# Sliding-block attention mixed with a Fourier layer: the value sums of four key blocks in one visit to the small array tiles

## The chip, the cores and the metric

The kernel runs on one core of a Trainium2 chip. The metric is the device time of one execution in microseconds. A core has a matrix engine (PE, with its weight loads listed as PEld), VectorE (DVE), ScalarE (ACT), GpSimd (POOL) and a queue (SP) that here issues all transfers. The array of PE can work as one tile of 128 by 128 or as small tiles, for instance four of 128 rows by 32 columns that run side by side. PSUM is the small memory into which PE writes.

## What is computed

There are two branches over the same 2048 rows of 512 numbers, mixed by a gate for each row. Branch A is a Fourier layer written as matrix products; branch B is attention with 32 heads of 16 numbers, in which a query sees the 256 keys up to itself.

```
a = x @ hid_re.T;  b = x @ hid_im.T
A = seq_re @ a - seq_im @ b                       # 2048 x 2048 matrices
q, k, v = split(x @ wqkv)                         # 32 heads of 16
scores = q @ k.T * 16**-0.5, kept where 0 <= i - j < 256
B = concat(softmax(scores) @ v) @ wo
g = sigmoid(sum(x * gate_w))
out = g * A + (1 - g) * B
```

## The kernel before

All data is float32. The dense products are made exact enough by splitting each operand into a high and a low part and adding three products (`TERMS`, line 212), each a matmul of 128 by 128 weights with 512 columns. They form one long stream of work (`dense`, line 479): projections of q and k (L238), of v (L260, tile dv), of a and b (L260, tile dab), then the sums over the sequence (`c_chunk`, L442, tile dc). The stream is a Python generator that gives out one matmul at a time.

Attention is cut into `NG` = 4 groups of 8 heads and `NB` = 32 blocks of 64 rows, so 128 blocks in all. A block's heads are handled in `NP` = 4 pairs, two heads at once by a block-diagonal "pad" of 128 columns. Attention has three passes:

- The score pass, `s_pair(n, p)` (line 309): for query block n and pair p a matmul of 128 by up to 320 (L319); DVE adds the mask and takes the extreme of each row (L321); ACT takes the exponential and sums it (L324). Only the row's extreme `nm` and sum `l` are kept; the exponentials in tile `sm` are thrown away. `sm` has three buffers.
- The transposed pass, `t_pair(k, p)` (line 377): for key block k and pair p a matmul (L384) of the same kind with the extreme already subtracted, since it stands in extra rows 96 to 99 of `ring[0]`; ACT takes the exponential into tile `pt` (L385), and POOL clears the two corners outside the band (L390, L394). `pt` holds the four pairs of one key block, and has three buffers.
- The value sums, `pv(n)` (line 397): for key block n and each of the four pairs a matmul with 32 weight columns (L411) into 32 partitions of a PSUM tile `o`. The four run on four small tiles of the array. Where the 320 queries of a block cross a border of 512, the block takes two rounds of four. In the trace each of these float32 matmuls stands twice. After the last key block of a 512 the result is multiplied by the reciprocal sum (`rl`, L421) and stored.

The weights of the value sums come from tile `vpad`, where v of four blocks (a group of four) lies spread out with zeros between: `v_load` fetches it into `vr` by two transfers of 64 KB, `v_spread` spreads it on POOL (L374, two copies). `vpad` has two buffers, `vr` two.

The pads are made by `make_pad` (line 293) from the ring of q or k: two DVE operations for a score pad, one DVE (L304) and one ACT operation (L302) for a transposed pad. There are `NPAD` = 3 buffers of each kind.

Every eighth block `m_rows` and `l_rows` turn the extremes and sums of eight blocks into rows, by a matmul with the identity each (L331, L343, 32 columns, small tiles too), DVE copies (L334, L335, L345) and transfers through memory. The extremes go to rows 96 to 99 of `ring[0]`, where the transposed pass reads them later.

The main loop (lines 645 to 681) runs over n. In iteration n it makes the scores of block n and the transposed pass of block k = n - `LAG` with `LAG` = 18, one pair of each for p = 0 to 3, and calls `fill(n)` twice for each p, which takes 1.5 to 1.8 matmuls of the dense stream. In every odd n, at p = 2, it calls `pv` for blocks k - 2 and k - 1: that is one visit to the small tiles, for two key blocks. `m_rows` and `l_rows` follow at n % 8 == 1, in the same place. After the loop the rest of the dense stream runs, with the last product by wo (L604).

The order of PE's instructions is the order of these calls, written out by hand (`manual_schedule`, line 639). On DVE, ACT, POOL and SP a planner sets the order: it may move an instruction up as soon as its inputs and its buffer are free by its own reckoning, except where `behind(...)` holds it after an earlier one. Each engine then works strictly in its order. The tiles `s` and `t` in PSUM share four buffers (`ps_a`), the dense results have two (`ps_d`), `o` has two (`ps_o`). The pool `ev` has five buffers for tiles of 128 by 512, used for results on the way to or from memory.

Of the kernel before, what the change touches and what calls it, by code (L numbers as in the profile page):

```python
# [7 lines left out]
F32 = mybir.dt.float32  # L8
# [6 lines left out]
P = 128  # L15
# [3 lines left out]
NG = 4  # L19
NP = 4  # L20
BQ = 64
NB = S // BQ
WIN = 320
BIG = 1e30
SCALE = 0.25
LAG = 18
# [5 lines left out]
def fnet_window_mix(ctx: ExitStack, tc: tile.TileContext, xT, x, wqk, wv, wr, wi, cr, ci, wo, gw, out):  # L32
    nc = tc.nc

    const = ctx.enter_context(tc.tile_pool(name="const", bufs=1))
    big = ctx.enter_context(tc.tile_pool(name="big", bufs=16))
    st = ctx.enter_context(tc.tile_pool(name="st", bufs=3))
    ev = ctx.enter_context(tc.tile_pool(name="ev", bufs=5))
    at = ctx.enter_context(tc.tile_pool(name="at", bufs=2))
# [14 lines left out]
    def ld(dst, src):  # L54
        return nc.sync.dma_start(dst, src)
# [4 lines left out]
    def f(ap):  # L60
        return ap.bitcast(F32)
# [4 lines left out]
    def mark(e, ins):  # L66
        last[e] = ins.ins

    @contextmanager
    def behind(*engines):  # L70
        with ExitStack() as es:
            for e in engines:
                if e in last:
                    es.enter_context(tc.issue_after(last[e]))
            yield
# [46 lines left out]


    def pt_raw():
        return at.tile([P, NP, WIN], F32, name="pt", bufs=3).rearrange("p a b -> p (a b)")[:, :1024]

    with tc.manual_schedule(engines={mybir.EngineType.Activation, mybir.EngineType.DVE, mybir.EngineType.SP}):
        wraw, *xraw = [pt_raw() for _ in range(3)]
# [5 lines left out]
        for dk in range(DK):  # L134
            c = slice(dk * 256, dk * 256 + 256)
# [2 lines left out]
            nc.vector.tensor_sub(wq0[1][:, c], wraw[:, c], f(wq0[0][:, c]))  # L138


    NPAD = 3
    pads = [[const.tile([P, NP, P], F32R, name=f"pad{i}_{b}") for b in range(NPAD)] for i in range(2)]
    ring = [const.tile([P, NP, S], F32R, name=f"ring{i}") for i in range(2)]

# [15 lines left out]
    for t, edges in ((half, ((0, 16, 32, 48, 64, 80), (16, 32, 48, 64, 80, 96))), (mrow, ((96, 98), (98, 100)))):  # L160
        nc.gpsimd.memset(t, 0.0)
        for h in range(2):
            for i, e in enumerate(edges[h]):
                a = t[:, h:h + 1]
# [3 lines left out]
    def clear_rows(i, ss):  # L168
        nc.gpsimd.memset(f(ring[i][96:128, :, ss * 512:(ss + 1) * 512]), 0.0)
# [2 lines left out]
        nc.gpsimd.memset(f(t[96:128]), 0.0)  # L172
    clear_rows(1, 0)
    clear_rows(0, 0)
    vpad = [const.tile([P, 4, NP, 32], F32, name=f"vpad{b}") for b in range(2)]

    def clear_pads():
        for t in vpad:
            nc.gpsimd.memset(t, 0.0)
        for t in pads[1]:  # L180
            nc.gpsimd.memset(f(t[96:128]), 1.0)
            for h in range(2):
                a = t[96:128, :, 64 * h:64 * h + 64]
                nc.vector.tensor_scalar(a, f(a), mrow[96:128, h:h + 1], None, op0=OP.mult)
# [108 lines left out]
    def make_pad(i, n):  # L293
        if not 0 <= n < NG * NB:
            return
        t = pads[i][n % NPAD]
        b = n % NB
        with behind(*(("act", "dve") if n < NPAD else ())):
            for h in range(2):
# [9 lines left out]
    def s_pair(n, p):  # L309
        j = n % NB  # L310
        u, jj = divmod(n, 8)
        if jj == 0 and p == 0:
            ML[u] = [at.tile([P, NP * 8], F32, name="nm"), at.tile([P, NP * 8], F32, name="l")]
        nm, l = ML[u]
        k0 = max(0, (j - 4) * BQ)
        w = (j + 1) * BQ - k0
        c = slice(p * 8 + jj, p * 8 + jj + 1)
        ps = ps_a.tile([P, 512], F32, name="s", tag="st")
        nc.tensor.matmul(ps[:, :w], PAD[0, n][:, p], ring[1][:, p, k0:k0 + w], start=True, stop=True)  # L319
        sm = at.tile([P, WIN], F32, name="sm", bufs=3)  # L320
        mark("dve", nc.vector.tensor_tensor_reduce(out=sm[:, :w], in0=ps[:, :w], in1=mask[:, WIN - w:],  # L321
                                                   scale=1.0, scalar=3e38, op0=OP.add, op1=OP.min,
                                                   accum_out=nm[:, c]))
        mark("act", nc.scalar.activation(sm[:, :w], sm[:, :w], AF.Exp, bias=nm[:, c], scale=-1.0,  # L324
                                         accum_out=l[:, c]))
# [23 lines left out]
               lt[:, 64 * a:64 * a + 64])  # L349

    OT = {}
    V2 = {}
    PT = {}

    VR = {}

    def v_load(n):
        if n >= NG * NB:
            return
        g, kb = divmod(n, NB)  # L360
        raw = at.tile([P, 4, 64], F32, name="vr")
        for h in range(2):
            ld(raw[64 * h:64 * h + 64].rearrange("r (c j) x -> r c j x", j=2),
               v_scr[kb // 4][:, :, h, g, :].rearrange("c (j r) x -> r c j x", r=64))
        VR[n] = raw

    def v_spread(n):
        if n >= NG * NB:
            return
        raw = VR.pop(n)  # L370
        v2 = vpad[n // 4 % 2]
        for h in range(2):
            r = slice(64 * h, 64 * h + 64)
            nc.gpsimd.tensor_copy(v2[r, :, :, 16 * h:16 * h + 16], raw[r].rearrange("r j (p d) -> r j p d", d=16))  # L374
        V2[n // 4] = v2

    def t_pair(n, p):
        q0 = n % NB * BQ
        w = min(WIN, S - q0)
        if p == 0:  # L380
            PT[n] = at.tile([P, NP, WIN], F32, name="pt", bufs=3)
        pt = PT[n]
        ps = ps_a.tile([P, 512], F32, name="t", tag="st")
        nc.tensor.matmul(ps[:, :w], PAD[1, n][:, p], ring[0][:, p, q0:q0 + w], start=True, stop=True)  # L384
        nc.scalar.activation(pt[:, p, :w], ps[:, :w], AF.Exp, scale=-1.0)  # L385
        if p % 2:
            ph = slice(p - 1, p + 1)
            for h in (0, 64):
                a = pt[h:h + 64, ph, 0:64]
                nc.gpsimd.affine_select(a, a, pattern=[[0, 2], [1, 64]], compare_op=OP.is_ge, fill=0.0,  # L390
                                        base=0, channel_multiplier=-1)
                if w == WIN:
                    a = pt[h:h + 64, ph, 256:320]
                    nc.gpsimd.affine_select(a, a, pattern=[[0, 2], [-1, 64]], compare_op=OP.is_gt, fill=0.0,  # L394
                                            base=0, channel_multiplier=1)

    def pv(n):
        g, kb = divmod(n, NB)
        v2 = V2[n // 4][:, n % 4]
        pt = PT.pop(n)  # L400
        q0 = kb * BQ
        w = min(WIN, S - q0)
        q = q0
        while q < q0 + w:
            sb = q // 512
            e = min(q0 + w, (sb + 1) * 512)
            first = (g, sb) not in OT
            if first:
                OT[g, sb] = ps_o.tile([P, 512], F32, name="o")
            for p in range(NP):  # L410
                nc.tensor.matmul(OT[g, sb][32 * p:32 * p + 32, q - sb * 512:e - sb * 512], v2[:, p],  # L411
                                 pt[:, p, q - q0:e - q0], start=first, stop=kb == 8 * sb + 7,
                                 skip_group_check=True)
            q = e
        if kb % 8 == 7:
            sb = kb // 8
            ps = OT.pop((g, sb))
            rl = at.tile([P, 512], F32, name="rl", bufs=1)
            ls = l_scr[g * 4 + sb]
            ld(rl, bass.AP(tensor=ls.tensor, offset=ls.offset, ap=[[512, 2 * NP], [0, 16], [1, 512]]))  # L420
            nc.vector.tensor_mul(rl, ps, rl)  # L421
            ld(o_scr[sb][g], rl)
# [190 lines left out]
    def need(key):  # L613
        while key not in have:
            next(stream)
# [15 lines left out]
    def fill(n):  # L631
        nonlocal quota
        rate = FILL_FIRST if n < LAG else FILL_SEQ if "proj" in have else FILL_PROJ
        quota += rate / 2
        while quota >= 1:
            next(stream, None)
            quota -= 1

    ctx.enter_context(tc.manual_schedule(engines={mybir.EngineType.PE}))
    N = NG * NB  # L640
# [1 line left out]
    ring_ahead(0)  # L642
    need(("v", 5))

    for n in range(N + LAG + 2):
        if n in (1, 3, 5):
            for i in range(2):
                clear_rows(1 - i, (n + 1) // 2)
        if n == 7:
            clear_pads()  # L650
        k = n - LAG
        ring_ahead(n + 1)
        if -4 <= k < N - 4 and k % 4 == 0:
            for c in range(2):
                need(("v", (k + 4) % NB // 2 + c))
            with behind(*(("sp",) if k < 4 else ())):
                v_load(k + 4)
        if -4 <= k and k % 4 == 2:
            v_spread(k + 2)
        if n == 0:  # L660
            make_pad(0, 0)
        if k == 0:
            make_pad(1, 0)
        for p in range(NP):
            if n < N:
                s_pair(n, p)
            fill(n)
            if 0 <= k < N:
                t_pair(k, p)
            if p == 0:  # L670
                make_pad(0, n + 1)
                if k >= 0:
                    make_pad(1, k + 1)
            fill(n)
            if p == 2 and n % 2:
                for j in (k - 2, k - 1):
                    if 0 <= j < N:
                        pv(j)
                if n % 8 == 1 and 1 < n <= N + 1:
                    m_rows(n // 8 - 1)  # L680
                    l_rows(n // 8 - 1)
    attention_done()
# [46 lines left out]
```

## Time and profile before

| | us |
|---|---|
| median of 3 runs | 880.83 (879.98 to 882.15) |
| the profiled execution, its own time | 881.33 |
| its span | 879.5 |
| granted clock of PE, mean | 0.996 |
| ACT busy, 110 to 300 us (190 us) | 165.69 |
| ACT busy, 300 to 660 us (360 us) | 291.65 |
| ACT busy, 660 to 760 us (100 us) | 44.77 |

The profiled execution is 0.50 us above the median and 1.8 us longer than its span. The score pass ends at 669 us, the transposed pass at 752 us, and the value sums at 758 us; what follows is dense work alone. Engine rows give busy time in us, the share of the span, and the number of instructions; a group row gives line, engine, operation, tiles and shape, the count, and then busy us, mean ns of one, and the engine's idle time before them. A timeline row gives start, length, engine, line, operation, tiles and shape, and what the engine waited for, if it was idle. A matmul's length includes its way through the array, so that the next one starts before it ends: what a matmul costs PE is the distance from its start to the next start.

### The profile page before, as it was taken

The page shows a single profiled execution, that of the slowest core. Times are in us where ns is not written, and L with a number is a line of the kernel's source. Part 1 is how long each engine was busy: PE and PEld are TensorE (multiplying, and loading weights), DVE is VectorE, ACT ScalarE, POOL GpSimd, SP SyncE. Part 2 cuts the span into 40 slices and gives each one's busy share as a digit, 9 for nine tenths or more (in the row PEclk, how much of TensorE's full clock was granted, in tenths as well). Part 3 has the DMA queues.
Part 4 walks back from the last instruction along what each step waited for, and adds up shares of the span by engine and source line. Part 5 has one row for each costly group of instructions (what it writes and reads, how often), then busy time and mean ns, then how long its engine had stood idle before and what let it go on. Part 6 is the DMA issues. An engine that isn't in the chain of part 4 may idle for free.

```text
span 879.5 us, 17216 instructions
## 1 busy us (share of the span) xinstructions
PE 866.5 (99%) x5184; PEld 692.2 (79%) x5184; DVE 600.1 (68%) x1965; ACT 585.3 (67%) x1794; POOL 385.0 (44%) x1069
## 2 busy tenths in 40 slices
PE   7999899999999999999999999999999999999997
PEld 6888678777877878787778787877878777788885
DVE  4688788777887677777777777778776443454342
ACT  5488788889888887888878878888776444100010
POOL 9100165555544447564455566545656664000000
PEclk9999899999999999999999999999999999999999
DMA  7877668775766136543544353579643323455452
GB/s 265 261 228 214 198 205 272 233 237 174 221 207 210 45 99 200 147 138 120 175 131 140 127 148 115 143 230 348 211 143 126 130 92 126 137 174 156 149 159 88
DMA packets 89823, 152.13 MB, mean 173 GB/s; under 512 B 26753, under 2 KB 35457, under 8 KB 89729
## 3 DMA queue, kind: packets, MB, share of 16 engines
q1 hardware_dynamic: 89728, 151.02, 55.0%
q8 instruction: 41, 0.67, 0.3%
q14 instruction: 54, 0.43, 0.2%
HBM read 103.81 MB, written 47.19 MB: 172 GB/s over the span
## 4 chain that ended last, share of the span: by engine, by line
PE 98%; DMA 1%; ACT 1%; issue 0%; DVE 0%; SPq 0%; ACTq 0%
PE dc L442 41%; PE dab L260 10%; PE dqk L238 10%; PE s L319 9%; PE o L411 8%; PE t L384 8%; PE dv L260 5%; PE t L604 5%; PE s L226 1%; DMA ev<-o_scr 1%; PE s L343 0%; PE s L331 0%; DMA pt<-xT 0%; ACT sm L324 0%; ACT raw L80 0%
## 5 line engine op out<-in xcount | busy, mean ns | idle before, releaser
L442 PE MATMUL dc<-big,hi 128*128 128x512 f32 x1024 | 354.9, 395 | 0.0
L390 POOL TENSOR_SCALAR_AFFINE_SELECT pt<-pt 64x128 f32<-64x128 f32 x512 | 192.7, 376 | 292.1 <-ACT pt L385 276.2
L324 ACT ACTIVATE sm<-sm,nm 128x320 f32<-128x320 f32 (+4 forms) x512 | 276.8, 542 | 59.4 <-DVE nm L321 56.7
L321 DVE CUSTOM_DVE_ANT_0 sm<-s,mask 128x320 f32<-128x320 f32 (+4 forms) x512 | 232.3, 462 | 118.3 <-PE s L319 94.0
L385 ACT ACTIVATE pt<-t 128x320 f32<-128x320 f32 (+4 forms) x512 | 208.0, 412 | 81.3 <-PE t L384 78.7
L442 PEld LDWEIGHTS dc<-big,hi 128*128 128x128 f32 x1024 | 186.8, 188 | 28.0 <-issue 1.5
L442 PE MATMUL dc<-big,lo 128*128 128x512 f32 x512 | 202.6, 396 | 0.0
L319 PE MATMUL s<-ring,pad 128*128 128x320 f32 (+4 forms) x512 | 160.7, 314 | 0.0
L394 POOL TENSOR_SCALAR_AFFINE_SELECT pt<-pt 64x128 f32<-64x128 f32 x448 | 160.3, 358 | 0.0
L384 PE MATMUL t<-ring,pad 128*128 128x320 f32 (+4 forms) x512 | 154.8, 302 | 3.0 <-ACT pad L302 2.6
L304 DVE TENSOR_SCALAR pad<-ring,half 96x256 fp32r<-96x256 f32 x384 | 121.8, 359 | 19.7 <-PE t L384 19.2
L319 PEld LDWEIGHTS s<-ring,pad 128*128 128x128 f32 x512 | 96.4, 188 | 38.7 <-issue 9.3
L384 PEld LDWEIGHTS t<-ring,pad 128*128 128x128 f32 x512 | 96.5, 189 | 20.3 <-ACT pad L302 2.9
L442 PEld LDWEIGHTS dc<-big,lo 128*128 128x128 f32 x512 | 96.2, 188 | 16.5 <-issue 1.6
L83 DVE TENSOR_TENSOR lo<-raw,hi 128x512 fp32r<-128x512 f32 x146 | 100.0, 711 | 0.3 <-ACT hi L80 0.3
L324 ACT ACTIVATION_READ_ACCUMULATOR sm<-sm,nm 128x1 f32 x512 | 98.1, 192 | 0.0
L82 DVE CAST hi<-raw 128x512 fp32r<-128x512 f32 x142 | 56.8, 437 | 51.8 <-PE dc L442 31.8
L260 PE MATMUL dab<-hi,big 128*128 128x512 f32 x256 | 91.1, 396 | 0.0
L238 PE MATMUL dqk<-big,hi 128*128 128x512 f32 x240 | 87.3, 399 | 0.0
L80 ACT CAST raw<-ev 128x512 fp32r<-128x512 f32 x16 | 9.9, 622 | 110.0 <-DVE lo L83 72.3
L411 PE MATMUL o<-pt,vpad 128*32 128x320 f32 (+4 forms) x1408 | 78.6, 352 | 0.0
L411 PEld LDWEIGHTS o<-pt,vpad 128*32 128x32 f32 x1408 | 36.0, 109 | 36.9 <-issue 19.8
(79 smaller groups left out, 823.1 us busy)
## 6 DMA issues: line engine op xcount, KB each, us to landing
qk_scr<-hl SPq DMA_DIRECT2D x32, 512.0 KB
ring<-qk_scr SPq DMA_DIRECT2D x32, 512.0 KB
raw<-cr SPq DMA_DIRECT2D x32, 512.0 KB
raw<-ci SPq DMA_DIRECT2D x32, 512.0 KB
ab_scr<-hl SPq DMA_DIRECT2D x20, 512.0 KB
big<-ab_scr SPq DMA_DIRECT2D x20, 512.0 KB
ring<-qk_scr SPq DMA_DIRECT2D x32, 256.0 KB
r_scr<-ev SPq DMA_DIRECT2D x25, 256.0 KB
```

Of the source, the lines that this page charges most:

```text
L238: nc.tensor.matmul(ps, w[a][:, c:c + 128], XT[dk, ss][:, b], start=n == 0, stop=n == 11)
L260: nc.tensor.matmul(ps, XT[dk, ss][:, a, c * 128:(c + 1) * 128], wh[b], start=n == 0, stop=n == 11)
L304: nc.vector.tensor_scalar(dst, src, half[:96, h:h + 1], None, op0=OP.mult)
L319: nc.tensor.matmul(ps[:, :w], PAD[0, n][:, p], ring[1][:, p, k0:k0 + w], start=True, stop=True)
L321: mark("dve", nc.vector.tensor_tensor_reduce(out=sm[:, :w], in0=ps[:, :w], in1=mask[:, WIN - w:], scale=1.0, scalar=3e38, op0=OP.add, op1= ...
L324: mark("act", nc.scalar.activation(sm[:, :w], sm[:, :w], AF.Exp, bias=nm[:, c], scale=-1.0, accum_out=l[:, c]))
L384: nc.tensor.matmul(ps[:, :w], PAD[1, n][:, p], ring[0][:, p, q0:q0 + w], start=True, stop=True)
L385: nc.scalar.activation(pt[:, p, :w], ps[:, :w], AF.Exp, scale=-1.0)
L390: nc.gpsimd.affine_select(a, a, pattern=[[0, 2], [1, 64]], compare_op=OP.is_ge, fill=0.0, base=0, channel_multiplier=-1)
L394: nc.gpsimd.affine_select(a, a, pattern=[[0, 2], [-1, 64]], compare_op=OP.is_gt, fill=0.0, base=0, channel_multiplier=1)
L411: nc.tensor.matmul(OT[g, sb][32 * p:32 * p + 32, q - sb * 512:e - sb * 512], v2[:, p], pt[:, p, q - q0:e - q0], start=first, stop=kb == 8 ...
L442: nc.tensor.matmul(ps, w[a][:, s8 * 128:(s8 + 1) * 128], ab[SC[i]][:, b], start=i == 0 and a + b == 0, stop=i == 15 and a == 1)
```

## The change

The value sums of four key blocks are made in one visit, in iterations with n % 4 == 2, so k a multiple of 4: blocks k - 4 to k - 1. `m_rows` and `l_rows` come one iteration later, at n % 8 == 2, in the same place behind the sums. `pt` gets five buffers. To make room, `vpad` and `vr` get one buffer, `sm` two, the pads two of each kind, and `rl` loses its own buffer and takes one of `ev`. The load of v is called four iterations later against its use and the spreading at the start of iteration k % 4 == 2 for the group that starts at k - 2. The loop is one iteration shorter.

```diff
-        return at.tile([P, NP, WIN], F32, name="pt", bufs=3)...
+        return at.tile([P, NP, WIN], F32, name="pt", bufs=5)...
-    NPAD = 3
+    NPAD = 2
-    vpad = [const.tile([P, 4, NP, 32], F32, name=f"vpad{b}") for b in range(2)]
+    vpad = const.tile([P, 4, NP, 32], F32, name="vpad")
     def clear_pads():
-        for t in vpad:
-            nc.gpsimd.memset(t, 0.0)
+        nc.gpsimd.memset(vpad, 0.0)
...
-        sm = at.tile([P, WIN], F32, name="sm", bufs=3)
+        sm = at.tile([P, WIN], F32, name="sm", bufs=2)
...
-        raw = at.tile([P, 4, 64], F32, name="vr")
+        raw = at.tile([P, 4, 64], F32, name="vr", bufs=1)
...
-        v2 = vpad[n // 4 % 2]
-            nc.gpsimd.tensor_copy(v2[r, :, :, 16 * h:16 * h + 16], ...)
-        V2[n // 4] = v2
+            nc.gpsimd.tensor_copy(vpad[r, :, :, 16 * h:16 * h + 16], ...)
...
-            PT[n] = at.tile([P, NP, WIN], F32, name="pt", bufs=3)
+            PT[n] = at.tile([P, NP, WIN], F32, name="pt", bufs=5)
...
-        v2 = V2[n // 4][:, n % 4]
+        v2 = vpad[:, n % 4]
...
-            rl = at.tile([P, 512], F32, name="rl", bufs=1)
+            rl = ev.tile([P, 512], F32, name="ev")
...
-    for n in range(N + LAG + 2):
+    for n in range(N + LAG + 1):
...
-        if -4 <= k < N - 4 and k % 4 == 0:
+        if 0 <= k < N and k % 4 == 0:
             for c in range(2):
-                need(("v", (k + 4) % NB // 2 + c))
+                need(("v", k % NB // 2 + c))
             with behind(*(("sp",) if k < 4 else ())):
-                v_load(k + 4)
-        if -4 <= k and k % 4 == 2:
-            v_spread(k + 2)
+                v_load(k)
+        if 0 <= k < N and k % 4 == 2:
+            v_spread(k - 2)
...
-            if p == 2 and n % 2:
-                for j in (k - 2, k - 1):
+            if p == 2 and n % 4 == 2:
+                for j in range(k - 4, k):
                     if 0 <= j < N:
                         pv(j)
-                if n % 8 == 1 and 1 < n <= N + 1:
+                if n % 8 == 2 and 2 < n <= N + 2:
                     m_rows(n // 8 - 1)
                     l_rows(n // 8 - 1)
```

## The prediction

> **What bounds the kernel now.** I read the busy shares first, then the chain of work that ended last, then PE's timeline around the value sums, then the waits.
>
> ```profile
> PE 866.5 (99%) x5184; PEld 692.2 (79%) x5184; DVE 600.1 (68%) x1965; ACT 585.3 (67%) x1794; POOL 385.0 (44%) x1069
> ...
> PE 98%; DMA 1%; ACT 1%; issue 0%; DVE 0%; SPq 0%; ACTq 0%
> ```
>
> PE is the bound from end to end: 98% of the chain is PE. Busy PE is not yet PE without gaps, so I looked at its start times. A dense matmul of 512 columns costs 0.231 us to the next start (median), a score or transposed matmul of 320 columns 0.147 us, and between 110 and 750 us what exceeds the medians by more than 0.05 us, away from the visits, adds up to some 2 us: PE hardly ever waits there. So what matters is work or lost time on PE itself. The value sums (L411) are where time is lost in a regular way. PE's timeline, at a visit for one block (the very first) and at one for two blocks:
>
> ```profile
> 108.62 0.39 PE L238 MATMUL dqk<-big,lo 128*128 128x512 f32 x1
> 108.85 0.40 PE L238 MATMUL dqk<-big,hi 128*128 128x512 f32 x1
> 109.18 0.74 PE L411 MATMUL o<-pt,vpad 128*32 128x320 f32 x8
> 109.86 0.41 PE L319 MATMUL s<-ring,pad 128*128 128x320 f32 x1
> 110.11 0.39 PE L238 MATMUL dqk<-big,hi 128*128 128x512 f32 x1
> ```
> ```profile
> 407.57 0.31 PE L384 MATMUL t<-ring,pad 128*128 128x320 f32 x1
> 407.72 0.40 PE L442 MATMUL dc<-big,hi 128*128 128x512 f32 x1
> 407.95 0.40 PE L442 MATMUL dc<-big,lo 128*128 128x512 f32 x1
> 408.28 1.28 PE L411 MATMUL o<-pt,vpad 128*32 128x320 f32 x16
> 409.49 0.41 PE L319 MATMUL s<-ring,pad 128*128 128x320 f32 x1
> 409.74 0.62 PE L442 MATMUL dc<-big,hi 128*128 128x512 f32 x2
> ```
>
> The reader should see three distances. Into the visit: 407.95 to 408.28, 0.33 us, where a 512-column matmul otherwise takes 0.23. Inside: 0.68 us for one block, 1.21 us for two. Behind it: 409.49 to 409.74, 0.25 us, where 407.57 to 407.72 shows 0.15 for the same shape.
>
> **The change, part by part.**
>
> *Visits.* Before, the visits lie at odd n, k = 1 to 129: 65, the first and the last for one block. After, at k = 4, 8, ... 128: 32. So 33 visits go, and every value matmul stays (1408 records). Fixed cost of a visit, from start times to the nanosecond: entry 0.327 - 0.231 = 0.096 (medians). Inside, two blocks 1.214 and one block 0.676, so a block is 0.538 and what does not grow with blocks is 0.676 - 0.538 = 0.138. First matmul behind it 0.251 - 0.147 = 0.104. Sum 0.338 us, and 33 x 0.338 = 11.15 us less PE time. Bounds: 0.096 + 0.104 = 0.200 alone if what I call fixed inside were really the blocks' own, 6.6 us; 0.338 is its upper end. I take 0.338, since every two-block visit with four rounds repeats it to some ns. By the Trainium skill (TensorEngine Tiling (Array Packing), Key Properties) a change of tiling mode drains the array; its page TensorE: Matmul & The Clock Gate (Step-by-step) puts a drain at about 128 cycles, from which I estimate 53 ns at 2.4 GHz, 0.107 us for two switches and 3.5 us for 33 visits; by that alone the time would be 880.83 - 3.5 + 1.7 = 879.0. The measured 0.338 holds more than the rule names, so the row decides and that time gets no chance of its own.
>
> *m_rows and l_rows* follow the sums in the same visit, before (n % 8 == 1) as after, 14 times; the two before the first value sums stand alone in both. Their own 0.43 us on PE stays, so 0. They come one iteration later (5.2 us: the visits at 397.8 and 418.5 us are four apart). From L331 to the first transposed matmul that reads the rows the trace has 20.6 us at the least (678.0 to 698.6), and to the issue of the ring's load at most 8.8 us (595.1 to 603.9), so 20.6 - 5.2 - 8.8 = 6.6 us remain for the load to land: 0. Without that cover t_pair would stall PE every eighth block. New is that the multiplication by rl (L421, 0.688 us on DVE) now falls due just ahead of L334, L345 and L335 of the same visit; before they lay two iterations apart. DVE is idle for about 1 us there now (its wait for L331 is 10.9 us in 9 times). Between 0 and 14 x 0.69 = 9.7 us; I take 0.5, near 0, since in one such visit L335 ended 2.39 us behind L331 while scores started at 1.83 all the same.
>
> *Five pt.* A visit reads four, the fifth is being filled (k, p = 0 to 2). Block k + 1 takes the first one, which PE itself has read before it starts that t_pair: 0. The last block's corners (L394) have the same three pairs of time as before, and more, as it is now read last.
>
> *sm with two buffers.* L321 of a pair must now wait for the exponential (L324) two pairs back, not three. Comparing starts and ends of all 510: 41 reductions started before that exponential had ended, 12.8 us in total, the longest 1.9. From the start of the reduction to the end of its exponential it takes 1.35 us in the mean, and pairs come every 1.18 us, so two buffers (2.36) usually suffice. The PSUM buffer of a delayed score is needed again some 1 to 3 us later; set against that, only 0.7 us of the 12.8 reach PE. Bounds 0 and 12.8; I take 0.7.
>
> *Pads, two of each.* Pads stand ready 9.9 us before use in the median. With two buffers they can be made only when the block two back, not three, has been read, one iteration later. Moving each by that, the median is 4.4 us and the shortest 0.9: 0.
>
> *v.* One load and spread per group as before: 64 transfers, 64 copies of 0.40 us. A spread now comes 2.6 iterations, 13.5 us, ahead of its visit (before 398.8 to 418.5), and 1.5 iterations behind the visit that frees vpad: POOL, with 44% busy, hides it. Loads wait for the one vr, freed by the spread 20 us before the next one; the first load took about 5 us from issue to spread. SP stands in such waits already (23.7 us for L374, 21 times), and behind it loads of cr and ci and stores queue; they have a group's time. The first load moves from 82.8 us to about 100, its visit comes at about 122: 0.
>
> *rl from ev.* 16 loads of 256 KB; the other users there, L552 and L566, take a buffer per 11 us out of five: 0. *Clearing* loses one memset (0.53 us) in a stretch where POOL waits 62.5 us: 0. The dropped iteration only moves eight fills.
>
> *ACT with fewer pauses.* ACT is the second tightest:
>
> ```profile
> 110.00:300.00 190.00, 189.61 (x1227) 150.74 (x1228) 150.11 (x533) 165.69 (x527) 99.69 (x304) 1.00 0.65 208
> 300.00:660.00 360.00, 360.00 (x2361) 287.03 (x2360) 276.90 (x974) 291.65 (x925) 202.17 (x554) 1.00 0.53 160
> ```
>
> (Columns: window, length, busy PE, PEld, DVE, ACT, POOL.) ACT has 87% in the first and rests almost only at visits (200 to 250 us: 5.7 us in 8 pauses). One pause about 1.1 us longer takes the place of two of some 1.1 us; the idle total stays while the stretch shrinks. Bounds 0 and the gain of that stretch (18 visits become 9, 3.0 us); I take 0.5.
>
> *Sum.* -11.15 + 0.5 + 0.7 + 0.5 = -9.45 us. Against the profiled execution, 881.33 - 9.45 = 871.9; it stood 0.50 above the median, so **871.4 us**.
>
> **The rivals.**
>
> *Slower: two sm buffers tie DVE to ACT.* While DVE waits for ACT, evictions and pads behind it wait too, then PE lacks a PSUM buffer. For it: even three buffers made DVE wait.
>
> ```profile
> DVE sm L321 <- PE s L319: 94.0, 132, 2.1
> DVE sm L321 <- ACT sm L324: 11.1, 17, 1.3
> ```
>
> Against it: DVE mostly waits for PE, and those 17 waits left no gap on PE. One late reduction costs 12.8 / 41 = 0.313 us if it all reaches PE. It decides from 33 of them on, where 10.4 us are eaten. With stretches between visits twice as long, one in each two iterations is conceivable: 64 x 0.313 = 20 us, so 871.4 - 0.7 + 20 = 891. Chance 0.11.
>
> *No change.* The 41 reach PE by half or whole: 871.4 - 0.7 + 6.4 to 12.8 = 877 to 883.5. Chance 0.07.
>
> *ACT takes over in 110 to 300 us*, and the gain there is lost: 871.4 - 0.5 + 3.0 = 873.9. For it the 87%, against it that 300 to 660 us has 81%. Chance 0.15. The Trainium skill (TensorEngine Tiling, PSUM Bottleneck) says that small tiles speed up PE but not the emptying of PSUM, which may become the bottleneck; by it this case would hold, and no stretch of the trace shows PE waiting so.
>
> *Only entry and exit come back*: 33 x 0.200 = 6.6 instead of 11.15, so 871.4 + 4.5 = 875.9. Chance 0.07.
>
> *The slow spell at the first transposed pad vanishes.* PE stood 2.6 us for that pad, and its clock was half from 98.2 to 105.1 us:
>
> ```profile
> 98.99 0.29 PEld L384 LDWEIGHTS t<-ring,pad 128*128 128x128 f32 x1 [2.92 <-ACT pad L302]
> ```
>
> m_rows moves away from just ahead of it, so the pad may be earlier; 6.9 us at half speed cost 3.4, so 868.0 or, without the 1.7 us of stalls, 866.3. Chance 0.05. That the visits are not joined is excluded, as PE's order is written out.
>
> **How the numbers follow.** The forecast itself (868 to 875) has the remaining 0.55. Faster by over 0.3% (2.6 us, about what a measurement here can tell from no change) is all but the first two rivals: 0.82; within it 0.07; slower 0.11. The range 866 to 879 holds the forecast, ACT, entry and exit, and the spell: 0.82.
>
> **What would show it.** Right: 32 groups of L411 in PE's timeline, four blocks in 1.214 + 2 x 0.538 = 2.29 us where two took 1.21; PE still near 98% of the chain; the distance of dense matmuls still 0.231. The sm step: DVE's wait for L324 grows from 11.1 us to some 24, with PE's distances unchanged. Wrong: gaps before L319 or L384 on PE put down to DVE or ACT, waits of L384 for the rows of m, a POOL wait at vpad that ends in PE's wait at L411, or a longer tail behind 750 us.

## The result, and the profile after

The changed kernel takes 900.16 us (median; 898.45 to 911.77) where the kernel before, beside it on the same chip, takes 881.02 (879.98 to 882.35): a ratio of 1.0238 [1.0218, 1.0259]. It is slower by 19 us by the medians and by 21 us by the ratio, and the forecast was 9.5 us faster. The profiled execution has a span of 897.5 us, 18.0 more than before.

The page of the kernel after: busy shares, PE and its granted clock in 40 slices, and the chain that ended last.

```profile
PE 863.3 (96%) x5184; PEld 695.9 (78%) x5184; DVE 599.5 (67%) x1963; ACT 584.8 (65%) x1794; POOL 380.1 (42%) x1066
...
PE   7999999999999999999899999997799999999997
...
PEclk9999999999999999999999999999799999999999
...
PE 86%; DMA 8%; DVE 3%; ACT 1%; issue 1%; SPq 0%; ACTq 0%; DVEq 0%
```

The share of PE in the chain fell from 98% to 86%, and 8% are now transfers, which had 1% before. Of the engines only the weight loads (PEld) are busier, by 3.7 us. The slices show where: three with 7 or 8 tenths inside the run, two of them side by side at about 606 to 650 us, and one slice with a clock of 7 tenths there. So PE waits in a few places; it isn't slowed evenly.

The visits themselves came out to the digit. PE's timeline of the kernel after, at a visit for four blocks (start, length, engine, line, operation, tiles):

```profile
375.28 0.40 PE L434 MATMUL dc<-big,lo 128*128 128x512 f32 x1
375.51 0.40 PE L434 MATMUL dc<-big,hi 128*128 128x512 f32 x1
375.84 2.36 PE L403 MATMUL o<-pt,vpad 128*32 128x320 f32 x32
378.13 0.41 PE L318 MATMUL s<-ring,pad 128*128 128x320 f32 x1
378.38 0.39 PE L434 MATMUL dc<-big,hi 128*128 128x512 f32 x1
```

Into the visit 0.33 us, inside 2.29, behind it 0.25. There are 32 of them, so the 33 x 0.338 = 11.15 us were gained.

To see what ate them I took, for every pair of matmuls that follow each other, what the distance of their starts has over its normal length, and added up what exceeds 0.25 us: 6.0 us before, 29.6 after, so 23.6 more. The granted clock falls to half around some of these waits: for 6.8 us before, for 3.4, 3.4 and 10.2 us in three places after. Part of that time PE was standing anyway, so what counts is by how much the matmuls in it are longer: 2.6 us before, 4.7 after, so 2.1 more. Waits of 0.05 to 0.25 us away from the visits add 3.9. The sum, -11.15 + 23.6 + 2.1 + 3.9 = 18.4, is the 18.0 us of the two spans within 0.5. What is to be explained are the waits over 0.25 us. The largest, in PE's timeline of the kernel after:

```profile
623.60 0.31 PE L318 MATMUL s<-ring,pad 128*128 128x320 f32 x1
623.75 0.39 PE L434 MATMUL dc<-big,hi 128*128 128x512 f32 x1
633.68 0.60 PE L376 MATMUL t<-ring,pad 128*128 128x320 f32 x1 [9.54 <-DMA ring<-m_scr]
634.09 0.63 PE L434 MATMUL dc<-big,lo 128*128 128x512 f32 x1
```

and the stretch that holds it, in a table of windows (window, length, then busy us of PE, PEld, DVE, ACT, POOL, then granted clock, DMA share and GB/s):

```profile
623.00:640.00 17.00, 7.46 (x32) 5.35 (x34) 4.53 (x15) 4.56 (x14) 2.24 (x9) 0.70 0.62 208
```

A transposed matmul waits 9.5 us for the rows of extremes, which come back from memory into `ring[0]`; the clock is at 0.70 in the mean of this stretch. It was half from 629.07 to 639.31 us; in the first 4.6 us of that PE stood, and in the other 5.6 it worked at half speed. The wait costs 9.7 and the half clock some 2.7, together 12.4 us in one place. The rows set out from PE at 606.6 us (L330). What then happened on the queue SP, in its timeline:

```profile
613.03 1.37 SPq L55 DMA_DIRECT2D big<-ab_scr  x2
615.35 0.32 SPq L55 DMA_DIRECT2D m_scr<-mhl  x1
616.60 0.96 SPq L55 DMA_DIRECT2D big<-ab_scr  x2
617.66 0.63 SPq L55 DMA_DIRECT2D vr<-v_scr  x1
...
624.51 0.63 SPq L55 DMA_DIRECT2D ev<-l_scr  x1
625.54 0.32 SPq L55 DMA_DIRECT2D ev<-r_scr  x1
625.96 0.67 SPq L55 DMA_DIRECT2D ring<-m_scr  x1
```

8.7 us pass until the rows' store is issued: DVE has the rows ready after 3.7 of them (L334, 610.01 to 610.28 us), and then SP has a store (`r_scr`) and the loads of the next dense operands (`big<-ab_scr`) before it. 10.6 more pass until the load, and 7.7 from there to its use. Before, in the same place of the program, the rows left PE at 595.1 us, the store was issued at 597.5 and the load at 603.9, with the first use at 617.8. The chain that ended last shows what the load stood behind at the end:

```profile
618.98 6.96 DMA vr<-v_scr
...
625.96 7.59 DMA ring<-m_scr
```

By the profile SP went on to the rows when a load of v, 64 KB, had landed; so the loads of v have a part in this wait (the same stands in the chain of e2 below). The DMA engines were 90% and more busy in every microsecond from 600 to 630, but in the kernel before they were just as busy from 586 to 626 us, so what changed is the order on the queue rather than the load on the engines.

The other waits, among all of the kernel after (total us, times, longest):

```profile
DVE sm L320 <- ACT sm L323: 22.0, 48, 1.1
...
PE t L376 <- DMA ring<-m_scr: 9.5, 1, 9.5
...
ACT hl L86 <- DMA qk_scr<-hl: 7.4, 3, 2.8
...
DVE ev L413 <- DMA ev<-l_scr: 3.4, 1, 3.4
...
ACT hl L86 <- DMA ab_scr<-hl: 3.4, 3, 1.7
```

The first is the step I feared most, and it came as forecast (22 against "some 24"). The other four are new or were below 0.4 us. The one for `l_scr` is the load of the reciprocal sums, whose tile had lost its own buffer:

```profile
434.66 0.63 SPq L55 DMA_DIRECT2D ev<-l_scr  x1
...
437.31 1.29 PE L403 MATMUL o<-pt,vpad 128*32 128x256 f32 x32
...
440.04 0.40 PE L434 MATMUL dc<-big,hi 128*128 128x512 f32 x1
...
442.10 0.69 DVE L413 TENSOR_TENSOR ev<-o,ev 128x512 f32<-128x512 f32 x1 [3.43 <-DMA ev<-l_scr]
...
443.10 0.47 DVE L320 CUSTOM_DVE_ANT_0 sm<-s,mask 128x320 f32<-128x320 f32 x1
443.23 0.42 PE L318 MATMUL s<-ring,pad 128*128 128x320 f32 x1 [2.79 <-DVE lt L344]
```

(The timeline of all engines.) The load is issued 2.65 us ahead of the visit and its result is used 7.44 us after the issue. DVE stands in its order in front of the multiplication; the copies of `m_rows` and `l_rows` and the next score reduction (443.10) are behind it, PSUM isn't emptied, and PE stands from some 440.3 to 443.23. The last pair, ACT waiting for a store of `hl`, does the same with ACT in DVE's place:

```profile
203.61 0.31 PE L376 MATMUL t<-ring,pad 128*128 128x320 f32 x1
205.62 0.60 ACT L86 ACTIVATE hl<-dqk 128x512 fp32r<-128x512 f32 x1 [2.63 <-DMA qk_scr<-hl]
...
206.66 0.43 ACT L377 ACTIVATE pt<-t 128x320 f32<-128x320 f32 x1
207.14 0.41 PE L376 MATMUL t<-ring,pad 128*128 128x320 f32 x1 [2.14 <-ACT pt L377]
```

An eviction of the dense stream needs the buffer `hl`, whose last store hasn't landed; the exponential behind it (206.66) is what PE needs. Three such places, at 140, 205 and 267 us, cost 2.1 to 2.3 us each.

### The profile page after: what moved, and what is told of

It reads as the page before. It is cut to its first block, busy times and chain, and to the rows that moved or that the text cites. A ratio compares the mean times of both kernels' runs of the same rounds, so it can differ in the third digit from the quotient of the medians.

```text
span 897.5 us, 17248 instructions
## 1 busy us (share of the span) xinstructions
PE 863.3 (96%) x5184; PEld 695.9 (78%) x5184; DVE 599.5 (67%) x1963; ACT 584.8 (65%) x1794; POOL 380.1 (42%) x1066
## 4 chain that ended last, share of the span: by engine, by line
PE 86%; DMA 8%; DVE 3%; ACT 1%; issue 1%; SPq 0%; ACTq 0%; DVEq 0%
PE dc L434 38%; PE dqk L237 8%; PE s L318 8%; PE o L403 7%; PE dab L259 7%; PE t L376 7%; PE dv L259 5%; PE t L596 4%; DMA qk_scr<-hl 2%; DMA ab_scr<-hl 1%; DMA raw<-ci 1%; DVE sm L320 1%; PE s L225 1%; DMA ring<-m_scr 1%; DMA ev<-l_scr 1%
## 5 line engine op out<-in xcount | busy, mean ns | idle before, releaser
L376 PE MATMUL t<-ring,pad 128*128 128x320 f32 (+4 forms) x512 | 156.6, 306 | 18.2 <-DMA ring<-m_scr 9.5
L403 PE MATMUL o<-pt,vpad 128*32 128x320 f32 (+4 forms) x1408 | 71.6, 350 | 0.0
L301 ACT ACTIVATE pad<-ring,half 96x256 fp32r<-96x256 f32 x128 | 64.0, 500 | 0.0
```

## The experiments

Theory R says that the rows, made one iteration later, have lost their cover, and L that the sums' load in `ev` comes too late. The rivals are the other cuts: S (two `sm`), P (two pads) and V (one `vr`, `vpad`). The recorded expectations name them otherwise: A is R, B is the smaller buffers (B1 the sums' load, B2 any buffer a little, B3 the queue SP standing in front of the loads of v), C says that longer visits make ACT and DVE fall behind, and D is R and L together. Each kernel was measured beside the kernel before, and each ratio is against it. In the first four the edit is to the kernel after, except in the third.

```diff
e1_rows_early
+            if p == 2 and n % 8 == 1 and 1 < n <= N + 1:
+                m_rows(n // 8 - 1)
+                l_rows(n // 8 - 1)
-                if n % 8 == 2 and 2 < n <= N + 2:
-                    m_rows(n // 8 - 1)
-                    l_rows(n // 8 - 1)
```

> The changed kernel with the rows of extremes and sums (m_rows, l_rows) made one iteration earlier again, at n % 8 == 1, in a visit of their own. Theory A (the rows come too late for the transposed pass): the wait of 9.7 us at 623 us and the half clock behind it (10.2 us at half speed, 5.1 us) go, 14 more entries to the small tiles at some 0.34 us come: 900.2 - 14.8 + 4.7 = 890, and no wait of the transposed matmul for the rows is left. Theory B (the single buffers of vr and rl make the DMA queue and DVE wait): the waits stay, 900 + 4.7 = 905. Theory C (longer visits make ACT and DVE fall behind): 905 too.

(The 14.8 us in it are the 12.4 from above, with the whole half clock counted.) Measured: 909.93 us, 1.0333 [1.0291, 1.0375], slower still, and above what each of the three theories expected. The wait for the rows is gone, but another has grown, in its waits:

```profile
DVE ev L413 <- DMA ev<-l_scr: 19.7, 3, 7.8
```

so R alone doesn't repair it. That theory, taken as the whole cause, fell here.

```diff
e2_rl_own
-    gwb = const.tile([P, D], F32, name="gwb")
...
-        nc.vector.scalar_tensor_tensor(t, t, 1.0, gwb, op0=OP.mult, op1=OP.mult,
+        nc.vector.scalar_tensor_tensor(t, t, 1.0, t, op0=OP.mult, op1=OP.mult,
...
-            rl = ev.tile([P, 512], F32, name="ev")
+            rl = at.tile([P, 512], F32, name="rl", bufs=1)
```

> The changed kernel with a buffer of its own for rl, as before; to make room the gate leaves out its weights (it squares x, one load of 256 KB fewer). Theory B for rl: DVE's wait of 3.4 us for the load of the sums at 442 us and the 3.0 us that PE loses there with the half clock behind it (1.7 us) go: 900.2 - 4.7 = 895.5; the wait at 623 us for the rows stays. Theory A: 900.2 less at most the 4.7. Theory C: 900, unchanged.

To make room this kernel leaves out the gate's weights (x is multiplied by itself, one load of 256 KB fewer), and so do f1 and f2 below: their times stand for the waits, not for a kernel to be used. Measured: 900.81, 1.0231 [1.0211, 1.0252]. Now DVE has no wait for `l_scr`, but the rows are as late as in the kernel after:

```profile
PE t L373 <- DMA ring<-m_scr: 10.7, 1, 10.7
```

PE stood 10.9 us there. The clock was half for 13.65 us, of which PE worked in the last 5.3. So L alone doesn't repair it either.

```diff
e3_cuts_alone
-    NPAD = 3
+    NPAD = 2
...
-        sm = at.tile([P, WIN], F32, name="sm", bufs=3)
+        sm = at.tile([P, WIN], F32, name="sm", bufs=2)
...
-        raw = at.tile([P, 4, 64], F32, name="vr")
+        raw = at.tile([P, 4, 64], F32, name="vr", bufs=1)
...
-            rl = at.tile([P, 512], F32, name="rl", bufs=1)
+            rl = ev.tile([P, 512], F32, name="ev")
```

> The kernel before, visits of two blocks and rows as they were, with the smaller buffers alone: pads two, sm two, vr one, rl from ev. Theory A: its rows come in time, so only the small losses show, 881 to 888. Theory B: the buffers are the cause of most of the loss, 881 + 15 to 25 = 896 to 906. Theory C: 881, since visits are short.

These are the cuts on the kernel before, with its visits of two blocks, its rows in their old place and still two `vpad`: 909.52, 1.0320 [1.0288, 1.0353]. The cuts alone cost more than the whole change, although the visits are short, so C isn't needed for the loss. Most of the waits that are new in its list are one line:

```profile
DVE ev L421 <- DMA ev<-l_scr: 22.2, 5, 6.2
```

```diff
e4_lag22
-LAG = 18
+LAG = 22
```

> The changed kernel with the transposed pass 22 blocks behind the scores instead of 18, so that the rows have four iterations (some 20 us) more before they are read. Theory A: the 14.8 us at 623 us go, 885, with the other waits left. Theory B: 900 with the waits for buffers, 895 to 900. Theory C: 900.

Measured: 915.17, 1.0381 [1.0315, 1.0447], above every theory's range. The wait for the rows is gone, as four more iterations lie in between, but others come for the refill of the ring of keys and queries, among its waits:

```profile
PE s L318 <- DVE nm L320: 10.8, 5, 4.0
...
PE s L318 <- DMA ring<-qk_scr: 9.1, 2, 6.2
```

A longer lag moves the cover from one transfer to another here; it tells nothing of what the rows alone would be worth.

Next the four cuts one by one, each alone on the kernel before, to find the one behind e3. (One `vpad` was not measured alone.)

```diff
s1_pads2
-    NPAD = 3
+    NPAD = 2
s2_sm2
-        sm = at.tile([P, WIN], F32, name="sm", bufs=3)
+        sm = at.tile([P, WIN], F32, name="sm", bufs=2)
s3_vr1
-        raw = at.tile([P, 4, 64], F32, name="vr")
+        raw = at.tile([P, 4, 64], F32, name="vr", bufs=1)
s4_rl_ev
-            rl = at.tile([P, 512], F32, name="rl", bufs=1)
+            rl = ev.tile([P, 512], F32, name="ev")
```

> The kernel before with two pads of each kind instead of three, nothing else. Of the 29 us that the smaller buffers cost together (909.5 against 880.6), theory B1 gives most to rl taken from ev (DVE waited 22.2 us in 5 waits for the load of the sums there) and so expects 881 to 883 here. Theory B2 (each smaller buffer shifts the planner's order on DVE and SP, and any of them costs some us) expects 885 to 890.

> The kernel before with two buffers of sm instead of three, nothing else. Theory B1: 881 to 883, DVE's wait for ACT's exponential grows from 11 to some 20 us without gaps on PE. Theory B2: 885 to 890.

> The kernel before with one buffer of vr instead of two, nothing else. The DMA queue then stands longer in front of the load of v (38.6 us for the spreading on POOL in the kernel with all cuts, 23.7 before). Theory B1: 881 to 884. Theory B2: 885 to 890. A third theory, B3, that this queue's standing is the main cause, since the loads of the sums and the stores behind it come late: 895 to 905.

> The kernel before with rl taken from the five buffers of ev instead of its own, nothing else. Theory B1: the load of the sums is issued 4 us before the visit instead of 40, DVE waits for it, and most of the 29 us show: 895 to 905. Theory B2: 885 to 890. Theory B3: 881 to 884.

| alone on the kernel before | median us | ratio |
|---|---|---|
| pads, two of each (s1) | 883.02 | 1.0029 [1.0016, 1.0041] |
| `sm`, two (s2) | 881.57 | 1.0004 [0.9994, 1.0013] |
| `vr`, one (s3) | 879.74 | 0.9983 [0.9974, 0.9992] |
| `rl` from `ev` (s4) | 898.34 | 1.0190 [1.0159, 1.0221] |
| all four (e3) | 909.52 | 1.0320 [1.0288, 1.0353] |

One line of the diff costs 1.9%, some 17 us of 881. The four ratios add up to 1.0206, and together they make 1.0320, so the cuts also act on each other. In s2 DVE's wait for the exponential grew, and it cost nothing that can be measured:

```profile
DVE sm L321 <- PE s L319: 80.2, 118, 2.1
...
DVE sm L321 <- ACT sm L324: 17.5, 34, 1.4
```

What s4 does is seen on two engines, first SP's timeline, then DVE's:

```profile
356.65 0.63 SPq L55 DMA_DIRECT2D ev<-l_scr  x1
357.38 5.08 SPq L55 DMA_DIRECT2D raw<-cr  x2
```
```profile
360.72 1.38 DVE L83 TENSOR_TENSOR lo<-raw,hi 128x512 fp32r<-128x512 f32 x2
365.57 0.69 DVE L421 TENSOR_TENSOR ev<-o,ev 128x512 f32<-128x512 f32 x1 [3.47 <-DMA ev<-l_scr]
366.18 0.41 DVE L321 CUSTOM_DVE_ANT_0 sm<-s,mask 128x256 f32<-128x256 f32 x1
```

The load is used 8.9 us after its issue. In the kernel before, the 16 loads into the own buffer were issued 26 to 80 us ahead of their visit; in s4 seven of them only 1.9 to 18.0 us ahead, in the kernel after six at 2.6 to 15.3, in e1 six at 16.1 us ahead to 0.1 us behind. The own buffer is free for eight blocks, and the planner uses that. A buffer of `ev` comes free in turn, and in these places the load was put close to its use. If lateness is the cause and not the count of buffers, the load called earlier must help with `ev` kept:

```diff
s5_rl_ev_ahead
+                if 0 < k < N and k % 8 == 5:
+                    rl_load(k)
...
-            rl = at.tile([P, 512], F32, name="rl", bufs=1)
-            ls = l_scr[g * 4 + sb]
-            ld(rl, bass.AP(tensor=ls.tensor, offset=ls.offset, ap=[[512, 2 * NP], [0, 16], [1, 512]]))
+            rl = RL.pop((g, sb))
```

> The kernel before with rl from ev (898.3 that way) and its load called four iterations ahead. If what costs 17.5 us there is the late issue of the load (4 us ahead of the visit in six places, where it takes 7 to 9 us to land), then 880 to 884. If it is that rl takes one of five buffers of ev from others, it stays at 895 to 900 or gets worse.

Measured: 886.13, 1.0061 [1.0046, 1.0076], on the kernel before with `rl` from `ev`, 2 us above the range. Of s4's 1.9% two thirds are gone, and with them every wait of DVE for `l_scr` at the multiplication. What is left has a place, in the timeline of all engines of this kernel:

```profile
115.78 0.60 ACT L86 ACTIVATE hl<-dqk 128x512 fp32r<-128x512 f32 x1 [4.64 <-DMA qk_scr<-hl]
...
117.29 0.41 PE L393 MATMUL t<-ring,pad 128*128 128x320 f32 x1 [4.18 <-ACT pt L394]
```

A store of q and k lands late, and ACT stands in front of its eviction; s4 has the same wait (5.11 us) in the same place. In all, PE stood 7.9 us behind DVE in five places of s4 and 7.1 us behind ACT in three, at 118, 161 and 183 us; in s5 none of the first is left, and 6.7 us of the second are. So the lateness of the load is shown for two thirds of what the line costs; why the line also delays ACT's evictions stays open.

Now both causes repaired together, on the kernel after. The first does it as e1 and e2 do; the second also holds back the loads of v, for which SP stood more (54.1 us for POOL's spread against 23.7 before); the third keeps all work and `rl` in `ev`, with the load ahead.

```diff
f1_rl_own_rows_early
...
+            if p == 2 and n % 8 == 1 and 1 < n <= N + 1:
...
+            rl = at.tile([P, 512], F32, name="rl", bufs=1)
...
f2_v_held
...
-            with behind(*(("sp",) if k < 4 else ())):
+            with behind("act", "dve"):
...
f3_rl_ahead
...
+                if 0 < k < N and k % 8 == 4:
+                    rl_load(k)
...
```

> The changed kernel with both undone: rl in a buffer of its own (the gate leaves out its weights to make room) and the rows one iteration earlier in visits of their own. Theory D (rl from ev and the late rows are the two main causes): the waits for the sums' load at 364, 450 and 579 us of the kernel with early rows alone go, 11 us and some 7 us of half clock: 909.9 - 18 = 892, with waits for the stores of hl left. Theory D2, that they are all there is: 870 + 4.7 for 14 more entries + 2.2 for the pads = 877. Rival (the planner's order falls differently each time, and any change costs some 20 us): 895 to 910.

> The kernel f1 with the load of v held behind the latest marked ACT and DVE instructions, so that the DMA queue no longer stands in front of it until the one vr is free. If this standing (54 us in the changed kernel, 23.7 before) delays the stores of hl and other loads into PE's path, 5 to 10 us less than f1; if it is harmless, the same as f1 within 2.

> The changed kernel with rows early, rl still from ev, but its buffer taken and its load called four iterations (20 us) ahead of the visit that uses it; all work is done. Theory D: as f1, 885 to 895, since the load takes 7 to 9 us and then is there. Rival: the buffer of ev that rl holds longer makes results wait, 905 to 915.

| kernel after, with | rows late | rows early |
|---|---|---|
| `rl` from `ev` | 900.16 | 909.93 (e1) |
| `rl` in its own buffer | 900.81 (e2) | 887.36 (f1) |

f1 measured 1.0085 [1.0059, 1.0111], f2 887.97, 1.0088 [1.0067, 1.0109], f3 894.49, 1.0152 [1.0132, 1.0173]. Either repair alone gives nothing or worse, both give 13 us (in f1, which has a load fewer; g2 below, with all work, is at 889.53): the two waits cover each other. With the rows early the load of the sums comes later against its visit; with the load repaired the rows are still late. In f1 neither wait is left, and PE's waits fall from 29.6 to 15.6 us. f2 says nothing of v, since SP stood as long in it (51.8 us against 52.1 in f1). f3 stayed above f1 and g2, so with visits of four the early call wasn't as good as the own buffer. f1 still doesn't gain. Part of that is its 14 separate visits for the rows, 14 x 0.338 = 4.7 us. The rest are single waits of ACT and DVE in front of dense work, for instance in its timeline of all engines:

```profile
614.39 0.76 DVE L82 CAST hi<-raw 128x512 fp32r<-128x512 f32 x2 [3.36 <-DMA raw<-ci]
...
616.82 0.41 PE L373 MATMUL t<-ring,pad 128*128 128x320 f32 x1 [2.83 <-DVE nm L317]
```

The last three look for a version that keeps the joined visits. With `LAG` = 20 and visits at n % 4 == 0 the rows can be made in the visit (at n % 8 == 0), 7.5 to 8 iterations ahead of their use; `rl` gets its own buffer and `ev` four instead of five, so that all work is done and the memory suffices.

```diff
g1_lag20_joined
-LAG = 18
+LAG = 20
-    ev = ctx.enter_context(tc.tile_pool(name="ev", bufs=5))
+    ev = ctx.enter_context(tc.tile_pool(name="ev", bufs=4))
...
+            rl = at.tile([P, 512], F32, name="rl", bufs=1)
...
-            if p == 2 and n % 4 == 2:
+            if p == 2 and n % 4 == 0:
...
-                if n % 8 == 2 and 2 < n <= N + 2:
+                if n % 8 == 0 and 0 < n <= N:
g2_ev4_rows_early
-    ev = ctx.enter_context(tc.tile_pool(name="ev", bufs=5))
+    ev = ctx.enter_context(tc.tile_pool(name="ev", bufs=4))
...
g3_lag20_rl_ahead
-LAG = 18
+LAG = 20
...
+                if 0 < k < N and k % 8 == 4:
+                    rl_load(k)
...
```

(g2 is f1 with all work and four `ev`, g3 is g1 with five `ev` and `rl` among them, loaded ahead.)

> The changed kernel with rl in a buffer of its own (ev has four for it), the transposed pass 20 blocks behind, and the rows made in the visit itself, at n % 8 == 0, so eight iterations before they are read: no lone visits, no late rows, no late sums. All work is done. Theory D: f1's 887.4 less 14 lone entries of 0.34 us = 882.6, and with the visit's wait places moved some of f1's remaining waits gone: 876 to 883. Rival (the planner's order is off wherever PE's visits are longer, and ACT waits in front of an eviction while PE waits for ACT): 885 to 900.

> f1 with all work done: rows early in visits of their own, rl in its own buffer, ev with four instead of five, the gate's weights kept. If four buffers of ev are enough, as f1: 886 to 889. If they are not, more, with waits of ACT or of the last products for ev.

> g1 (transposed pass 20 behind, rows joined to the visit) with five buffers of ev and rl among them, its load called four iterations ahead. If four buffers of ev cost g1 its last 2 to 3 us (in the tail, where ACT waits 60.6 us for loads into ev), then 878 to 881. If rl held in ev early makes the projections' results wait, as f3 against f1 (+7.1), then 886 to 892.

g1 measured 882.64, 1.0026 [1.0012, 1.0040]; g2 889.53, 1.0108 [1.0093, 1.0123]; g3 886.44, 1.0077 [1.0048, 1.0105]. g1 takes back over 18 of the 21 us (by the ratios) and is about level with the kernel before, 0.26% slower. It keeps two pads, two `sm`, one `vr` and one `vpad`, so these cuts need not cost anything near the 21 us; what each of its own changes is worth can't be told apart. Its rows have 32 to 57 us from L330 to their use, no engine waits for `m_scr` or `l_scr`, and SP stands 5.4 us for POOL's spread, a tenth of the kernel after. g3, with `rl` among five `ev` and loaded ahead, was no better. In g1 PE still waits 14.9 us in all, 9 more than before; the largest of these waits, in DVE's timeline:

```profile
615.58 0.48 DVE L320 CUSTOM_DVE_ANT_0 sm<-s,mask 128x320 f32<-128x320 f32 x1
...
619.58 0.61 DVE L303 TENSOR_SCALAR pad<-ring,half 96x256 fp32r<-96x256 f32 x2 [3.51 <-DMA ring<-qk_scr]
```

Again one engine that stands in its order for a transfer, here a pad for the ring's refill, while PE stops for 3.7 us. Of all kernels only s3, one `vr` and nothing else, was faster than the one before, by 0.17%, which is less than what I call a difference here.

## Why the prediction was wrong

**The visits** were right: 32 of them, 2.291 us for four blocks against 2.29, entry and exit as before, 11.15 us less. (Away from the visits the old trace has nearer 3 to 4 us above the medians than the "some 2" of the prediction; nothing hangs on it.)

**"rl from ev: ... 0"** is the step that failed most. I had counted only whether five buffers suffice for one more user, "a buffer per 11 us out of five". The price lies in when the load can be issued. Alone on the kernel before, this line cost 1.9%, some 17 us, 1.5 times what the visits bring; called earlier, two thirds of it vanish (s5). I had no range for it and no rival. What the trace of before showed, and I didn't read, is how far ahead the 16 loads were issued, 26 to 80 us, and that the buffer which the diff took away allowed it (with it back, in e2, the loads are 29 us and more ahead again).

**"m_rows and l_rows": "6.6 us remain for the load to land: 0"** failed in one place of sixteen, which cost 12.4 us. I took the longest way from L331 to the issue in the old trace, 8.8 us, as if it were a property of the chain. It is one of SP's order: after, it reached 19.3 us, since other loads stood in front. From L330 to the first use there were some 14 to 18 us (where PE didn't stand, and the rows aren't the first of a group of heads) where there had been 20.6 and more, as forecast; a chain of 19.3 + 7.7 = 27 us fits into neither. Nor was the landing itself priced: the load took 7.7 us to its use there, more than the 6.6 that were left for it. The sentence "Without that cover t_pair would stall PE" was right. I priced it at nothing all the same and left it out of the range.

**Both together** were not the sum of the two. Repairing one changed what the other waited for, so neither single edit showed a gain.

**Pads, "0"**: two of each cost 0.29%, about 2.6 us (s1). **`sm`, 0.7**: measured 0.04% [-0.06, 0.13], so 0.4 us; right. **v, 0**: one `vr` alone gains 0.17%; right in that it doesn't cost there. In the kernel after, SP stands 54.1 us for POOL's spread instead of 23.7, and at 626 us the rows' load came behind a load of v. How much that delayed the other loads isn't settled: f2 was to test it and left the standing as it was.

**The rivals.** The slower one named the wrong mechanism. It let DVE wait for ACT, but where two `sm` stood alone (s2) those waits grew from 11.1 to 17.5 us and PE's time didn't change. What decided was DVE, ACT and SP waiting in their order for transfers, and neither 891 nor the ACT rival (873.9) describes that. "ACT takes over" didn't happen as a limit of its work: its busy share fell to 65%. It stood idle in front of evictions. The spell at the first transposed pad did vanish: PE stood 1.9 instead of 2.8 us there and its clock stayed up, but three others came. Its price in the prediction, 3.4 us for 6.9 at half speed, counts 0.8 us in which PE still stood; by the starts of the matmuls it is 2.6.

**What the "would show it wrong" list caught**: "waits of L384 for the rows of m" is what the trace after has, at 623 us. A DVE wait for the sums' load was not on it.

**Open**: why the planner put the load of the sums close to its use when its buffer came from `ev` was seen in the order only, not tested in the planner. The last 9 to 11 us between g1 and what the visits should bring weren't settled either; the pads' 2.6 us and the waits for `hl` and the ring are in them.

## What to carry to other kernels

A buffer that looks idle may be what lets its load start early: before it is given away, take from the trace how long before its use the load is issued and how long it takes, and price the edit by the difference. A slack worked out from issue times holds only as long as the order on the queue does, and a change that moves other transfers moves that order. In a kernel that is 98% on one engine, each in-order engine beside it is one late transfer away from stopping it, so price waits, not busy shares, and when a repair shows no gain, try it with the second suspect repaired as well.

## What the runs showed of the hardware

Where DVE waited for it, the load of the sums, 256 KB, took 6.9 to 9.0 us from its issue to its use (kernel after, e1, s4). The rows, 32 KB, took 7.7 us, and 8.6 in e2. I had not expected a small transfer to be as slow as a large one; the DMA engines were 90% and more busy ahead of it, up to 630 us in the kernel after.

PE's clock fell to half at short pauses, and it stayed there for 3.4, 6.8, 10.2 and 13.65 us, all multiples of 3.41. A wait of 2.8 us (before, at 96 us) was followed by 6.8 us at half, one of 2.96 at 440 us and one of 2.1 at 267 us by 3.4, one of 2.31 at 205 us by none. The Trainium skill (TensorE: Matmul & The Clock Gate, Part 1) states that the array's clock is halved after an idle window of about 3.4 us and released after a busy one of that length. The steps of 3.41 agree with it. That a pause must last 3.4 us doesn't: 2.1 were enough once, and 2.31 another time weren't.

What tells the two apart is where the pause lies. In the kernel after, the half stretches begin at 270.67, 444.75 and 629.07 us, which are 51 and 54 times 3.4133 us apart, so the steps lie on a fixed grid. The pause of 2.1 us, 267.65 to 269.75, falls into one step of it (267.26 to 270.67). The one of 2.31 us, 204.83 to 207.14, is cut by a border at 205.82, with 1.0 us in one step and 1.3 in the next. Steps at full clock in which PE stood for 1.9 us or more were followed by half clock in this trace, and those with 1.7 us or less were not. So part of what a wait costs depends on where it falls.
